# Attention and a gated convolution on one core: row sums inverted in 128 rows, last keys turned by DVE, jobs ordered by due times alone

## The chip, the cores and the metric

One core of a Trainium2 chip runs one program. The metric is the device time of one execution in microseconds; the time of a kernel is the median of its runs. The engines are TensorE (PE, with PEld for its weight loads), VectorE (DVE), ScalarE (ACT), GpSimd (POOL) and SyncE (SP), whose queue issues nearly all DMAs here.

## The reference

```python
# q, k, v: 8 batches x 8 heads x 576 x 64, float32
scores = matmul(rotate(q), rotate(k).T) / sqrt(64)
attn = exp(scores - max(scores))
attn = attn / (sum(attn) + 1e-9)
x = matmul(attn, v)                          # -> 8 x 576 x 512
gate_pre[:, s] = sum(conv_w[t] * x[:, s + t - 4] for t in range(5))
out = (1 / (1 + exp(-gate_pre)) * (x @ w_val)) @ w_out
```

## The kernel before, in words

The work is cut into 32 pairs: two heads of one batch side by side in the 128 partitions. Four pairs make a batch; then the gated block of this batch follows, in two halves of 288 positions and four chunks of 128 columns.

A pair goes through these stages. `load` brings queries and keys with their swapped halves into the single tiles `qin` and `kin`. `rope_mul` (two products with the tables), `rope_add`, `qk_hi` (a cast) and `qk_lo` (a difference) turn them into a high and a low part. `s_mm` computes the scores in five chunks c: chunks 0 to 3 have 128 queries for each of the two heads, chunk 4 is the mixed one, with the last 64 queries of both heads. For each of the nine score tiles `s_max` (DVE) takes the negative maximum into `nm`, and `s_exp` (ACT) the exponential, whose row sum goes into a column of `sums`. The exponentials have queries in partitions; the product with the values needs keys there, so they are turned.

For the first pairs (p < EARLY) and the last one PE transposes them (`t_mm`), and ACT or DVE copies the result (`t_copy`). For the others DVE transposes 32 x 32 blocks (`turn`, eight a pair, 512 keys each) into a staging tile T, and sixteen DMAs (`move`) carry the blocks to their places in the tile P. T and P come from the three buffers `big`. The last 64 of the 576 keys of both heads are transposed by PE in every pair (`th_mm`, four transposes) and copied into `pl` by `h_copy`. The mixed tile `pm` is turned by PE (`tm_mm`, `hm_mm`) and copied into `pq` by `m_copy` and `hm_copy`; `hm_mm` also transposes the row sums, to 16 rows of 128.

`r_inv` adds 1e-9 and inverts them on these 16 rows, `r_write` stores them in DRAM (`rd`), and `r_read` reads them back, spread over 64 partitions (`rb`). `pv_mm` and `pvm_mm` multiply by the values, `x_norm` and `xm_norm` multiply by the inverses. Then `x_hi`, `x_lo`, the five taps of the convolution (`tap`: the first on ACT, four on DVE), and `gate`. The gated block is `f_mm` for both matrices, with `y_mul`, `y_hi`, `y_lo` between them and `o_out`, `o_dma` at the end. The weights and taps come as 64-bit floats and are decoded at the start (`decode`).

What sets the order: every step is a job with a due time, an engine, an estimated duration, and the tokens that it reads and writes. The due time is a base, counted from the start of the pair in a period of 18.0, plus a number from the table DUE. `Plan.order` walks the jobs with estimated durations: for each engine it looks at the jobs that can start within a short time of the earliest, takes the one with the smallest due time, and of the engines' choices the earliest start. This gives one sequence of jobs, and each engine gets its part of it in this order. PICK says which engine does a job that several can do. Each engine works strictly in its row.

## Time and profile before

| what | us |
|---|---|
| median of 3 runs | 727.49 (727.17 to 730.32) |
| profiled execution, time | 730.04 |
| its span, first to last instruction | 728.2 |
| PE, DVE, ACT, POOL busy in it | 653.0, 630.7, 464.7, 423.3 |
| normalization of pair 4 starts | 153.40 |
| normalization of pair 30 starts | 677.85 |

The span is shorter than the execution's time by what lies before the first and after the last instruction. Busy time of an engine is the time in which it had at least one instruction running. In a row of the groups view, the numbers after the first bar are the busy time in us and the mean of one instruction in ns, and after the second bar the idle time of the engine just before these instructions, with what ended it. Line numbers are those of the kernel before; a name such as `ps_t` stands for all buffers of that tile.

### The profile page before, as it was taken

The numbers are of one execution on the slowest core, as the hardware profiler recorded it, in microseconds if no ns is written. First come the engines' busy times: TensorE is split into PE (matmuls) and PEld (weight loads), VectorE is DVE, ScalarE is ACT, GpSimd is POOL, SyncE is SP. The second block draws the span as 40 slices with busy tenths as digits, with TensorE's granted clock in tenths as the row PEclk, the third lists the DMA queues.
The fourth block names the chain that finished last, engine by engine and source line by source line (L and its number), as shares of the span: only waits on it lengthen the run. The fifth ranks groups of instructions, "written<-read, shape, count | busy, mean of one in ns | idle before, by whom it ended". The sixth has DMA issues, their size and how long they took to land.

```text
span 728.2 us, 14173 instructions
## 1 busy us (share of the span) xinstructions
PE 653.0 (90%) x5044; PEld 473.2 (65%) x5044; DVE 630.7 (87%) x980; ACT 464.7 (64%) x1125; POOL 423.3 (58%) x312
## 2 busy tenths in 40 slices
...
GB/s 257 66 130 186 30 101 129 114 154 220 231 226 217 206 214 195 214 213 216 225 205 186 211 203 184 213 202 214 232 222 175 221 184 222 215 187 153 49 33 66
DMA packets 52245, 129.63 MB, mean 178 GB/s; under 512 B 11184, under 2 KB 21200, under 8 KB 52176
## 3 DMA queue, kind: packets, MB, share of 16 engines
...
## 4 chain that ended last, share of the span: by engine, by line
PE 37%; DVE 31%; DMA 13%; ACT 6%; SPq 6%; issue 5%; POOL 2%; DVEq 0%; ACTq 0%; POOLq 0%
PE ps_t L472 13%; PE ps_t L377 9%; DVE nm L275 9%; PE ps_s L269 8%; DVE g L446 6%; DVE big L304 6%; SPq L309 4%; DMA kin<-in_k 4%; ACT p L288 3%; DMA v<-in_v 3%; DMA big<-big 3%; PE ps_t L380 3%; DMA rb<-rd 2%; DVE kin L233 2%; DVE rr L399 1%
## 5 line engine op out<-in xcount | busy, mean ns | idle before, releaser
L288 ACT ACTIVATE p<-ps_s,nm 128x576 f32<-128x576 f32 x256 | 188.1, 739 | 79.1 <-DVE nm L275 76.6
L275 DVE TENSOR_REDUCE nm<-ps_s 128x1 f32<-128x576 f32 x288 | 204.2, 738 | 23.4 <-PE ps_s L269 22.4
L269 PE MATMUL ps_s<-k,q 64*128 64x288 f32 x1536 | 152.0, 320 | 20.2 <-ACT k L244 8.9
L269 PEld LDWEIGHTS ps_s<-k,q 64*128 64x128 f32 x1536 | 116.6, 193 | 52.2 <-issue 21.0
L304 DVE STREAM_TRANSPOSE big<-p 128x512 f32<-128x512 f32 x216 | 142.4, 685 | 6.1 <-ACT p L288 5.9
L233 POOL TENSOR_TENSOR qin<-qin,tab 128x576 f32<-128x576 f32 x59 | 87.5, 1497 | 70.4 <-DMA qin<-in_q 64.3
L446 DVE SCALAR_TENSOR_TENSOR g<-x,cw,g 128x576 f32<-128x576 f32 (+1 forms) x132 | 125.6, 956 | 1.9 <-ACT g L443 1.7
L377 PE MATMUL ps_t<-big,v 128*64 128x512 f32 (+2 forms) x528 | 119.4, 586 | 5.5 <-DMA rd<-rr 3.2
L472 PE MATMUL ps_t<-yh,wout_hi 128*128 128x288 f32 x256 | 81.2, 317 | 4.9 <-ACT pl L213 1.8
L472 PE MATMUL ps_t<-xh,wval_hi 128*128 128x288 f32 x256 | 80.1, 313 | 3.1 <-DVE g L477 2.0
L237 POOL TENSOR_TENSOR kin<-kin 128x576 f32<-128x576 f32 (+1 forms) x32 | 51.0, 1594 | 45.9 <-DVE kin L233 38.8
L472 PE MATMUL ps_t<-yh,wout_lo 128*128 128x288 f32 x256 | 77.5, 303 | 0.0
L472 PE MATMUL ps_t<-yl,wout_hi 128*128 128x288 f32 x256 | 77.4, 302 | 0.0
L472 PE MATMUL ps_t<-xl,wval_hi 128*128 128x288 f32 x256 | 76.8, 300 | 0.0
L472 PE MATMUL ps_t<-xh,wval_lo 128*128 128x288 f32 x256 | 76.5, 299 | 0.0
L377 PEld LDWEIGHTS ps_t<-big,v 128*64 128x64 f32 x528 | 36.1, 136 | 62.1 <-issue 56.4
L433 POOL TENSOR_TENSOR xl<-x,xh 128x576 fp32r<-128x576 f32 (+1 forms) x32 | 51.5, 1608 | 41.6 <-ACT xh L429 39.9
L485 POOL TENSOR_TENSOR yl<-g,yh 128x288 fp32r<-128x288 f32 x56 | 47.2, 843 | 34.9 <-ACT yh L481 34.8
L248 POOL TENSOR_TENSOR q<-qin,q 128x576 fp32r<-128x576 f32 (+1 forms) x32 | 49.2, 1536 | 31.3 <-ACT q L244 31.3
L233 POOL TENSOR_TENSOR kin<-kin,tab 128x576 f32<-128x576 f32 x34 | 52.5, 1547 | 14.5 <-DMA kin<-in_k 14.5
L248 POOL TENSOR_TENSOR k<-kin,k 128x576 fp32r<-128x576 f32 x31 | 45.8, 1479 | 23.0 <-ACT k L244 21.9
L472 PEld LDWEIGHTS ps_t<-yh,wout_hi 128*128 128x128 f32 x256 | 49.2, 192 | 10.4 <-DVE g L477 2.6
...
## 6 DMA issues: line engine op xcount, KB each, us to landing
big<-big SPq DMA_DIRECT2D x432, 128.0 KB
...
```

The source lines that it names most:

```text
L233: eng.tensor_tensor(out=t[:, i, a:b], in0=t[:, i, a:b], in1=tabs[:, i, a:b], op=ALU.mult)
L237: eng.tensor_tensor(out=t[:, 0], in0=t[:, 0], in1=t[:, 1], op=ALU.add)
L248: eng.tensor_tensor(out=t[:, 1], in0=ins[n][:, 0, a:b], in1=t[:, 0].bitcast(F32), op=ALU.subtract)
L269: T.matmul(out=ps[:, half, 0:288], lhsT=st["q"][rows, x, c * 128:c * 128 + 128] if c < 4 else mixq[p % 2][:, x], rhs=st["k"][rows, y, k0:k ...
L275: V.tensor_reduce(out=st[f"nm{i}"], in_=st[f"s{i}"], axis=AX.XY, op=ALU.max, negate=True)
L288: A.activation(out=pd.rearrange("p (b x) -> p b x", b=2), in_=st[f"s{i}"], func=AF.Exp, bias=st[f"nm{i}"], scale=1.0, accum_out=sums[p % 2 ...
L304: V.transpose(out=t[:, :, cs.index(c), h].rearrange("p b k i -> p k b i"), in_=st[f"p{c}"][:, h, h * D:h * D + M].rearrange("p (k b i) -> ...
L377: T.matmul(out=acc[HEAD[h], 0:n], lhsT=st["v"][:, j, h, :], rhs=st["pt"][:, :, c0:c1, h, j].rearrange("p a c i -> p c a i"), start=(j == 0 ...
L433: eng.tensor_tensor(out=st["xl"][:, a:b], in0=xs[p % 2][:, 4 + a:4 + b], in1=st["xh"][:, a:b].bitcast(F32), op=ALU.subtract)
L446: V.scalar_tensor_tensor(out=g, in0=x_sb[:, a + k:b + k], scalar=w, in1=g, op0=ALU.mult, op1=ALU.add)
L472: T.matmul(out=acc[:, 0:n], lhsT=wt[w][:, kc, ds], rhs=mv, start=(kc == 0 and i == 0), stop=(kc == NCH - 1 and i == 2))
L485: eng.tensor_tensor(out=ffn[b, "l", dc, lo], in0=y, in1=ffn[b, "h", dc, lo].bitcast(F32), op=ALU.subtract)
```

## The change

1. `r_inv` works on the sums where they are, as nine columns in 128 partitions, and writes the inverses into columns 576 to 584 of `pm`, which is now a constant tile of 640 columns. `hm_mm` transposes columns 512 to 639, so the last keys of the mixed tile and the inverses are turned together; the transpose of `sums` is gone. `hm_copy` copies 96 rows to `pq`, now on DVE instead of ACT, and `r_write` reads the inverses from `pq`.
2. `turn` of the second head takes 640 columns instead of 512, so the last keys of both heads go through DVE and the moves as a ninth block of the tile P. A move carries 1152 elements a row instead of 1024. `th_mm` and `h_copy` stay only for the pairs that PE turns. `pl` and `rr` are gone.
3. `order` keeps no estimate of time: jobs whose inputs have been issued lie in a heap by their due time, and one whose buffer is not free is parked until one is. DUE has new numbers; the period is 18.5.
4. EARLY is 5 instead of 4. `yh` and `yl` have 7 buffers each instead of 8. One step of the weight decoding becomes an absolute value on ACT. PICK moves, among others, the key product with the cosine table (`kmul0`) from DVE to POOL and the output eviction `od1` from ACT to DVE.

```diff
-EARLY = 4
+EARLY = 5
-DUE = {'c0': 223.82, 'c0e': 343.31, ...
-PICK = {... 'chm': 'A', ... 'kmul0': 'V', ... 'od1': 'A', ...
+DUE = {'taps': -379.65, 'dtap': 4.77, ...
+PICK = {... 'chm': 'V', ... 'kmul0': 'G', ... 'od1': 'V', ...
-    BUFS = {"p": 3, "pm": 1, "big": 3, "pl": 2, "pq": 1, ... "yh": 8, "rb": 2, "rr": 1, "yl": 8, ...
+    BUFS = {"p": 3, "pm": 1, "big": 3, "pq": 1, ... "yh": 7, "rb": 2, "yl": 7, ...
     def order(self):
...
+        heap = [(jobs[i][0], i) for i in range(len(jobs)) if not left[i]]
+        heapify(heap)
         done = []
+        while heap:
+            i = heappop(heap)[1]
             got = []
             for inst in allocs[i]:
                 if inst not in self.slot:
                     tag = inst.split("/")[0]
+                    idle = [(freed.get(held, -1), k) for k, held in enumerate(slots[tag])
+                            if (tag, k) not in [g[1:] for g in got] and not to_come.get(held)]
+                    if not idle:
+                        parked[tag].append(i)
+                        break
+                    got.append((inst, tag, min(idle)[1]))
...
+    pm = const.tile([128, S + D], F32, name="pm")
...
-            st["pt"] = get(f"big/P{p}", [128, 4096]).rearrange("p (a c h k i) -> p a c h k i", a=4, c=4, h=2, k=4)
+            st["pt"] = get(f"big/P{p}", [128, 4608]).rearrange("p (a c k i) -> p a c k i", a=4, c=4, k=9)
...
+        k0, k1 = ((0, 4), (4, 9))[h]
+        V.transpose(out=t[:, :, cs.index(c), k0:k1].rearrange("p b k i -> p k b i"),
+                    in_=st[f"p{c}"].rearrange("p h s -> p (h s)")[:, k0 * 128:k1 * 128].rearrange("p (k b i) -> p k b i", b=4, i=32))
...
     def hm_mm(p):
-        T.transpose(out=st["bhm"][:, 0:128], in_=st["pm"][:, 448:S], identity=ident)
-        T.transpose(out=st["bhm"][0:16, 128:256], in_=sums[p % 2], identity=ident)
+        T.transpose(out=state[p]["bhm"][:, 0:128], in_=pm[:, M:S + D], identity=ident)
     def hm_copy(p, eng):
-        cast(eng, mixed(p)[D:128, M:M + 128], st["bhm"][D:128, 0:128])
+        cast(eng, mixed(p)[0:D + 32, M:M + 128], st["bhm"][0:D + 32, 0:128])
...
     def r_inv(p):
-        V.tensor_scalar(out=r, in0=st["bhm"][0:16, 128:256], scalar1=1e-9, scalar2=None, op0=ALU.add)
-        V.reciprocal(out=r, in_=r)
+        r = sums[p % 2][:, 0:9]
+        V.tensor_scalar(out=r, in0=r, scalar1=1e-9, scalar2=None, op0=ALU.add)
+        V.reciprocal(out=pm[:, S:S + 9], in_=r)
     def r_write(p, part):
-            SP.dma_start(out=st["rd"][0, 0:9 * 128]..., in_=st["rr"][0:9])
+            SP.dma_start(out=st["rd"][0, 0:9 * 128]..., in_=st["pq"][D:D + 9, M:M + 128])
...
-            lambda: V.tensor_scalar(out=hi, in0=hi, scalar1=0x7FF00000, scalar2=None, op0=ALU.bitwise_and),
+            lambda: A.activation(out=fh, in_=fh, func=AF.Abs) if eng else
+            V.tensor_scalar(out=hi, in0=hi, scalar1=0x7FF00000, scalar2=None, op0=ALU.bitwise_and),
...
-    PERIOD = 18.0
+    PERIOD = 18.5
```

Three places show how the rows of the engines change. The first is DVE's row in the middle of the run, around the inversion of one pair. `rr` are the turned sums, `big` the staging tile T, `p` the exponentials; L304 is `turn`, L275 `s_max`, L477 `y_mul`, L233 the key product `kmul0`, L446 a tap. Before:

```order
L398 TENSOR_SCALAR rr_3410<-ps_t_3411 16x128
L399 RECIPROCAL rr_3410<-rr_3410 16x128
L304 STREAM_TRANSPOSE big_3414<-p_3400 128x4x4x32
L275 TENSOR_REDUCE nm_3447<-ps_s_3416 128x1
L275 TENSOR_REDUCE nm_3459<-ps_s_3417 128x1
L477 SCALAR_TENSOR_TENSOR g_2858<-g_2858,ps_t_3441 128x288
L304 STREAM_TRANSPOSE big_3414<-p_3461 128x4x4x32 x2
L477 SCALAR_TENSOR_TENSOR g_2595<-g_2595,ps_t_3466 128x288
L233 TENSOR_TENSOR kin<-kin,tab 128x576
L446 SCALAR_TENSOR_TENSOR g_3379<-x_84,cw,g_3379 128x576
```

The same place in DVE's row after the change, where L356 and L357 are `r_inv`, L404 a tap, L376 and L380 `x_norm` and `xm_norm` of the pair before, L265 `turn`, L235 `s_max`, L435 `y_mul` and L175 the copy `hm_copy`:

```order
L356 TENSOR_SCALAR sums_87<-sums_87 128x9
L357 RECIPROCAL pm<-sums_87 128x9
L404 SCALAR_TENSOR_TENSOR g_3321<-x_85,cw,g_3321 128x576
L376 TENSOR_TENSOR x_84<-ps_t_3468,rb_3464 128x512
L265 STREAM_TRANSPOSE big_3544<-p_3532 128x4x4x32
L235 TENSOR_REDUCE nm_3560<-ps_s_3546 128x1
L380 TENSOR_TENSOR x_84<-ps_t_3564,rb_3464 128x64
L235 TENSOR_REDUCE nm_3611<-ps_s_3547 128x1
L265 STREAM_TRANSPOSE big_3544<-p_3532 128x5x4x32
L435 SCALAR_TENSOR_TENSOR g_2548<-g_2548,ps_t_3580 128x288
L175 COPY pq_3616<-ps_t_3617 96x128
```

The inversion has moved from behind PE's transpose to ahead of it, the copy follows nine rows later, every second transpose is the longer one, and the key product is no longer in the row.

The second place is PE's row around the transposes of one pair: L269 is `s_mm`, L332 `th_mm`, L361 and L362 `hm_mm`, L344 `tm_mm`. Before:

```order
L269 MATMUL ps_s_2316<-k_71,q_73 128x288
L332 MATMUL ps_t_2335<-ident,p_2207 128x128
L332 MATMUL ps_t_2335<-ident,p_2257 128x128
L361 MATMUL ps_t_2345<-ident,pm_2279 128x128
L362 MATMUL ps_t_2345<-ident,sums_85 16x128
L344 MATMUL ps_t_2356<-ident,pm_2279 128x128 x4
L269 MATMUL ps_s_2365<-k_71,q_73 128x288
```

After, with L430 `f_mm`, L321 `hm_mm` and L229 `s_mm`:

```order
L430 MATMUL ps_t_6164<-yl_5803,wout_hi 128x288
L430 MATMUL ps_t_6164<-yh_5802,wout_lo 128x288
L430 MATMUL ps_t_6164<-yh_5722,wout_hi 128x288
L430 MATMUL ps_t_6164<-yl_5723,wout_hi 128x288
L430 MATMUL ps_t_6164<-yh_5722,wout_lo 128x288
L321 MATMUL ps_t_6188<-ident,pm 128x128
L229 MATMUL ps_s_6195<-k_70,q_72 128x288
```

Of the transposes around the scores one is left here, between a block of `f_mm` and the next scores; the four of `tm_mm` follow after these scores.

The third place is POOL's row, which rotates queries and keys: L233 is `rope_mul`, L237 `rope_add`, L248 `qk_lo`, L433 `x_lo`, L485 `y_lo`. Before:

```order
L233 TENSOR_TENSOR qin<-qin,tab 128x576 x2
L237 TENSOR_TENSOR qin<-qin 128x576
L233 TENSOR_TENSOR kin<-kin,tab 128x576
L433 TENSOR_TENSOR xl_4488<-x_84,xh_4487 128x576
L248 TENSOR_TENSOR q_72<-qin,q_72 128x576
L237 TENSOR_TENSOR kin<-kin 128x576
L485 TENSOR_TENSOR yl_4544<-g_3935,yh_4543 128x288
L248 TENSOR_TENSOR k_70<-kin,k_70 128x576
```

After, where the same functions are L193, L197, L208, L391 and L443:

```order
L193 TENSOR_TENSOR qin<-qin,tab 128x576 x2
L193 TENSOR_TENSOR kin<-kin,tab 128x576 x2
L197 TENSOR_TENSOR kin<-kin 128x576
L197 TENSOR_TENSOR qin<-qin 128x576
L208 TENSOR_TENSOR k_71<-kin,k_71 128x576
L208 TENSOR_TENSOR q_73<-qin,q_73 128x576
L391 TENSOR_TENSOR xl_4180<-x_85,xh_4179 128x576
L391 TENSOR_TENSOR xl_4184<-x_84,xh_4183 128x576
L443 TENSOR_TENSOR yl_4165<-g_2845,yh_4164 128x288
```

Both key products now stand in POOL's row, and the product for xl has moved behind the rotation.

More of the change, by code (lines that the diff above doesn't have):

```diff
@@ L1 @@
 from contextlib import ExitStack
+from heapq import heapify, heappop, heappush
 import numpy as np
@@ L36 @@
 class Plan:
[L39 to L43 removed]
+    BUFS = {"p": 3, "pm": 1, "big": 3, "pq": 1, "xh": 5, "xl": 5, "g": 5, "yh": 7, "rb": 2, "yl": 7, "oo": 3, "rd": 2,
+            "ps_s": 3, "ps_t": 2, "nm": 4}
@@ L45, in __init__, with add @@
     def __init__(self):
         self.jobs = []
-    def add(self, due, engine, ns, fn, *args, r="", w="", kb=0, mode=None, port=False, hold=False):
-        self.jobs.append((due, engine, ns, fn, args, r.split(), w.split(), kb * 3.6, mode, port or engine == "G", hold))
+    def add(self, due, engine, fn, *args, r="", w=""):
+        self.jobs.append((due, engine, fn, args, r.split(), w.split()))
     def graph(self):
@@ L80, in graph, with order @@
         return [len(d) for d in deps], outs, allocs, uses
-    def order(self, due=None):
+    def order(self):
         jobs = self.jobs
-        n = len(jobs)
-        due = due or [j[0] for j in jobs]
         left, outs, allocs, uses = self.graph()
-        ready = [1000 * due[i] if jobs[i][10] else 0.0 for i in range(n)]
-        start, end = [None] * n, [0.0] * n
-        free = dict.fromkeys(self.LAG, 0.0)
-        open_jobs = {e: [] for e in free}
-        to_come, freed, self.slot = {}, {}, {}
+        to_come, freed, self.slot, self.before = {}, {}, {}, {}
         for u in uses:
@@ L95, in order @@
         slots = {tag: [None] * k for tag, k in self.BUFS.items()}
-        for i in range(n):
-            if not left[i]:
-                open_jobs[jobs[i][1]].append(i)
+        parked = {tag: [] for tag in slots}
+        heap = [(jobs[i][0], i) for i in range(len(jobs)) if not left[i]]
+        heapify(heap)
         done = []
-        moving = port = 0.0
-        mode = None
-        def earliest(i):
-            job = jobs[i]
-            t = max(ready[i], free[job[1]])
-            if job[9]:
-                t = max(t, port)
+        while heap:
+            i = heappop(heap)[1]
             got = []
@@ L161, in order @@
-        self.start, self.end = start, end
+                    idle = [(freed.get(held, -1), k) for k, held in enumerate(slots[tag])
[4 more added lines that the diff above has]
+                    got.append((inst, tag, min(idle)[1]))
+            else:
+                for inst, tag, k in got:
+                    self.slot[inst], self.before[inst] = k, slots[tag][k]
+                    slots[tag][k] = inst
+                for inst in uses[i]:
+                    to_come[inst] -= 1
+                    freed[inst] = len(done)
+                    if not to_come[inst]:
+                        tag = inst.split("/")[0]
+                        for j in parked[tag]:
+                            heappush(heap, (jobs[j][0], j))
+                        parked[tag] = []
+                done.append(i)
+                for o in outs[i]:
+                    left[o] -= 1
+                    if not left[o]:
+                        heappush(heap, (jobs[o][0], o))
@@ L162, in order @@
+        assert len(done) == len(jobs), "no job can start"
         return done
@@ L343, in tm_mm @@
         for j in range(4):
-            T.transpose(out=st["bm"][:, j * 128:(j + 1) * 128], in_=st["pm"][:, j * 128:(j + 1) * 128], identity=ident)
+            T.transpose(out=st["bm"][:, j * 128:(j + 1) * 128], in_=pm[:, j * 128:(j + 1) * 128], identity=ident)
     def mixed(p):
@@ L527, in load_taps @@
         tmp = get("oo/taps1", [128, G1])[:, 0:NCH * TAPS]
-        taps.extend(decode(st, tmp, V, whole=cw))
+        taps.extend(decode(st, tmp, whole=cw))
     wsteps, wstage = {}, {}
@@ L547, in attn_gated_ffn, with at @@
             V.memset(x_sb[:, 0:4], 0.0)
-        for s_ in sums:
-            V.memset(s_, 1.0)
+        V.memset(pm, 0.0)
         for t in mixq:
             V.memset(t.bitcast(F32), 0.0)
-    def at(key, base, e, ns, fn, *args, pick=None, **kw):
+    def at(key, base, e, ns, fn, *args, pick=None, r="", w="", kb=0, mode=None, port=False):
+        options = ns if pick else None
         if pick:
-            options = ns
             e = PICK.get(pick, e)
-            ns, kw["port"] = options[e]
+            ns, port = options[e]
             args = [ENG[e] if a == "ENGINE" else a for a in args]
-        plan.add(base + DUE.get(key, 0.0), e, ns, fn, *args, **kw)
+        plan.add(base + DUE.get(key, 0.0), e, fn, *args, r=r, w=w)
         if collect is not None:
-            collect.append((key, base, pick, options if pick else None))
+            collect.append((key, base, pick, options, ns, kb * 3.6, mode, port or e == "G"))
     def toks(f, *ranges):
@@ L578, in attn_gated_ffn @@
     for i in range(7):
-        at("dtap", 16 + 0.4 * i, "V", 150, lambda i=i: taps[i](), w="cw oo/taps0 oo/taps1", port=i in (1, 3, 5, 6), hold=True)
+        at("dtap", 16 + 0.4 * i, "V", 150, lambda i=i: taps[i](), w="cw oo/taps0 oo/taps1", port=i in (1, 3, 5, 6))
     def weights(n):
```

156 lines of the change are left out of this document (50 added, 106 removed).

## The prediction

> **What bounds the kernel now.** I read the page's engine totals first, then its chain, then the busy time in the stretch where the pairs run at an even pace.
>
> ```profile
> PE 653.0 (90%) x5044; PEld 473.2 (65%) x5044; DVE 630.7 (87%) x980; ACT 464.7 (64%) x1125; POOL 423.3 (58%) x312
> PE 37%; DVE 31%; DMA 13%; ACT 6%; SPq 6%; issue 5%; POOL 2%; DVEq 0%; ACTq 0%; POOLq 0%
> 153.40 0.69 DVE L418 TENSOR_TENSOR x<-ps_t,rb 128x512 f32<-128x512 f32 x1
> 677.85 0.69 DVE L418 TENSOR_TENSOR x<-ps_t,rb 128x512 f32<-128x512 f32 x1 [3.09 <-PE ps_t L380]
> 153.40:677.85 524.45, 497.31 (x3933) 358.17 (x3934) 472.21 (x726) 357.43 (x881) 342.46 (x253) 0.99 0.78 206
> ```
>
> The first row is the page's first part, the second its chain. The two L418 rows, from the timeline, are the normalization of pair 4 and of pair 30 (the fifth and the thirty-first to be normalized). Between them lie 26 pairs, so a pair takes 524.45 / 26 = 20.17 us. The last row is that stretch in the windows view: PE, PEld, DVE, ACT and POOL busy, the granted clock, the DMA share and GB/s. DVE is busy 472.21 of 524.45 us (90%), PE 497.31 (95%), POOL 342.46 (65%). No engine alone is the bound: the chain goes back and forth between PE and DVE, with loads between. So I cost both, and then ask whether POOL or a load is next.
>
> **DVE, part by part.** These rows, grouped by shape, carry the terms.
>
> ```profile
> L399 DVE RECIPROCAL rr<-rr 16x128 f32<-16x128 f32 x32 | 30.1, 941 | 1.1
> L398 DVE TENSOR_SCALAR rr<-ps_t 16x128 f32<-16x128 f32 x32 | 8.8, 274 | 5.0 <-PE ps_t L362 2.8 <-ACT pq L213 1.6 <-DMA v<-in_v 0.3
> L511 DVE TENSOR_SCALAR oo<-oo 128x20 int32<-128x20 int32 x1 | 0.2, 167 | 0.0
> L549 DVE MEMSET sums<- 128x16 f32 x2 | 0.1, 72 | 0.0
> L304 DVE STREAM_TRANSPOSE big<-p 128x512 f32<-128x512 f32 x216 | 142.4, 685 | 6.1 <-ACT p L288 5.9
> L233 DVE TENSOR_TENSOR kin<-kin,tab 128x576 f32<-128x576 f32 x28 | 25.9, 926 | 3.5 <-DMA kin<-in_k 3.5
> L418 DVE TENSOR_TENSOR x<-ps_t,rb 128x128 f32<-128x128 f32 x1 | 0.3, 292 | 0.4 <-PE ps_t L380 0.4
> L493 DVE TENSOR_SCALAR oo<-ps_t 128x288 f32<-128x288 f32 x4 | 1.8, 458 | 7.0 <-PE ps_t L472 7.0
> L509 DVE TENSOR_SCALAR big<-big 128x512 int32<-128x512 int32 x8 | 3.5, 437 | 0.0
> L215 DVE CAST k<-k 64x128 fp32r<-64x128 f32 x4 | 2.4, 591 | 0.1
> L215 DVE COPY pl<-ps_t 128x256 f32<-128x256 f32 x4 | 1.6, 412 | 1.4 <-PE ps_t L332 1.4
> L237 DVE TENSOR_TENSOR qin<-qin 128x576 f32<-128x576 f32 x3 | 3.4, 1147 | 0.0
> ```
>
> - Inversion: 32 x (0.941 + 0.274) = 38.9 us leave; 32 pairs of instructions on 128x9 come. No row shows that shape. The bounds are the 72 ns of a 128x16 memset and the 274 ns of L398; I take 167 ns each, from the 128x20 row, the nearest in shape with arithmetic. That is 10.7 us, net -28.2 (-34.3 to -21.4).
> - Transposes: 216 of 512 elements become 104 of 512 and 104 of 640. Eight go with pair 4, which now takes the PE route: -5.5. The longer form is between 685 ns (a fixed cost) and 856 (in proportion); I take 856, since 685 for 512 leaves little room for a fixed part: +17.8. Net +12.3 (-5.5 at the least).
> - The key product with the cosine table (`kmul0`): of 28 on DVE 8 stay: 20 x 0.926 = -18.5.
> - The copy of the turned mixed tail (`chm`) comes from ACT: 32 x 0.292 (L418's 128x128 form, also read from PSUM) = +9.3.
> - Output evictions: 4 become 16: 12 x 0.458 = +5.5.
> - Start and end: eight mask steps of the weight decoding (-3.5), four key casts (-2.4), four copies to pl (-1.6) and three adds of qin (-3.4) leave; four adds of kin (+4.6 at 1.147), a product (+1.2) and three evictions (about +1.5) come: -3.6.
>
> The sum is -28.2 + 12.3 - 18.5 + 9.3 + 5.5 - 3.6 = -23.2 us.
>
> **The port that DVE shares with POOL.** What leaves DVE lands on POOL: 20 products at 1.547 us, 30.9 us (the few adds that change places nearly cancel), so 423.3 becomes some 452 us (+6.8%). What POOL does is not free for DVE.
>
> ```profile
> L233 POOL TENSOR_TENSOR kin<-kin,tab 128x576 f32<-128x576 f32 x34 | 52.5, 1547 | 14.5 <-DMA kin<-in_k 14.5
> L446 DVE SCALAR_TENSOR_TENSOR g<-x,cw,g 128x576 f32<-128x576 f32 x124 | 121.7, 983 | 1.9 <-ACT g L443 1.7
> 494.60 0.77 DVE L446 SCALAR_TENSOR_TENSOR g<-x,cw,g 128x576 f32<-128x576 f32 x1
> 18.23 1.37 DVE L508 SCALAR_TENSOR_TENSOR oo<-oo,oo 128x20 int32<-128x20 int32 x1
> ```
>
> A tap can take 0.77 us; twenty elements, beside a POOL instruction, took 1.37. So the mean of 983 ns holds 213 ns of waiting, 26.4 us over 124 taps. With POOL work 6.8% up in a span some 3% shorter this grows by a tenth: +2.6. DVE's account becomes -20.6.
>
> The Trainium skill, page "SBUF — State Buffer", section "Who interferes with whom", says that a DVE instruction with two SBUF inputs and a GpSimd instruction shut each other out for the whole instruction. By it every two-input instruction waits on average half of a POOL instruction (0.7 us) times POOL's share, which rises by about 0.08; for 124 taps and as many other two-input instructions at most that is an estimated +14 us, and the forecast would be some 11 us later. The 20 elements that took 1.37 us agree with the rule; the mean tap, which waits 0.21 us and not 0.7 x 0.65 = 0.46, says that it is met half as often.
>
> **PE.** 104 of the 128 transposes of the last keys (L332) and all 32 of the row sums (L362) leave; 32 for pair 4 (L318) come. The matmuls that use the last keys stay, now out of the big tile.
>
> ```profile
> L332 PE MATMUL ps_t<-ident,p 128*128 128x128 f32 x128 | 28.8, 304 | 18.0 <-ACT p L288 11.3 <-DVE x L422 4.7 <-DVE rr L398 0.7
> L318 PE MATMUL ps_t<-ident,p 128*128 128x128 f32 x160 | 28.4, 322 | 10.5 <-DVE x L418 4.5 <-ACT big L213 2.4 <-DVE big L215 1.7
> L362 PE MATMUL ps_t<-ident,sums 128*16 128x128 f32 x32 | 9.0, 281 | 0.0
> L332 PEld LDWEIGHTS ps_t<-ident,p 128*128 128x128 f32 x128 | 14.1, 144 | 30.1 <-ACT p L288 12.4 <-issue 5.8 <-DVE x L422 4.5
> L318 PEld LDWEIGHTS ps_t<-ident,p 128*128 128x128 f32 x160 | 21.0, 163 | 17.2 <-ACT big L213 4.9 <-DVE x L418 4.6 <-DVE big L215 2.4
> L362 PEld LDWEIGHTS ps_t<-ident,sums 128*16 128x16 f32 x32 | 3.0, 93 | 0.0
> ```
>
> By PE's busy time this is -104 x 0.225 + 32 x 0.178 - 9.0 = -26.7 us; by the weight loads beneath it -104 x 0.110 (14.1 us for 128) + 32 x 0.131 - 3.0 = -10.3. I take the larger end, since the first row also has 18.0 us in which PE stood idle ahead of these transposes, and that wait goes with them; it is not in the sum.
>
> The Trainium skill, page "Perfetto Trace Analysis", section "Identifying the Most-Contended Engine", holds matmul busy time for a bad measure of how full TensorE is, and LDWEIGHTS busy time for a good one. By it PE is 65% full, its term is -10.3, and the weighted sum below would be -16 instead of -23. The chain, which puts 37% on PE, speaks against taking it for slack.
>
> **ACT, the row-sum path, buffers and DMA.**
>
> ```profile
> L213 ACT COPY pl<-ps_t 128x256 f32<-128x256 f32 x60 | 22.1, 368 | 13.8 <-PE ps_t L332 13.4
> L213 ACT COPY pq<-ps_t 64x128 f32<-64x128 f32 x32 | 8.4, 262 | 6.8 <-PE ps_t L362 4.3 <-DVE rr L398 1.9
> 304.40 1.96 DMA rd<-rr
> 450.29 4.54 DMA rb<-rd
> big<-big SPq DMA_DIRECT2D x432, 128.0 KB
> ```
>
> ACT loses these two groups (30.5 us) and 12 output evictions, and gains the evictions of pair 4 and the decoding steps; it carries 6% of the chain, so I count nothing for it. The inverse now goes DVE, PE, DVE, SP instead of PE, DVE, SP: a copy more. On DVE the copy stands nine rows behind the inverse, and behind it wait taps and maxima if PE is late; on SP the write of the inverses waits for it, and behind that stand the next key load, the value load and the reads of the inverses. What hides it: the normalization that needs the inverses stands 24 DVE rows, at 472.21 / 726 = 0.65 us each some 16 us, behind the copy, against 1.96 + 4.54 us for write and read in the longer cases on the chain. If that cover is gone, DVE waits in every pair for what exceeds it. Nothing is counted. One buffer fewer for yh and yl binds only the eighth group of a batch, after the output matmuls that free the first have been issued; nothing again. The 416 moves carry 144 KB instead of 432 with 128 KB: 4.6 MB more of 129.63. With a shorter span the DMA share goes from 0.78 to some 0.83, which is room left, but loads may land later (a rival).
>
> **The sum.** DVE -20.6, PE -26.7. They take turns on the chain, 31 to 37, so I weight them: (31 x 20.6 + 37 x 26.7) / 68 = 23.9, rounded down to 23, since some of the gain will meet the next wait. Against the profiled execution: span 728.2 - 23 = 705.2, and with the 1.84 us that lie outside the span (730.04 - 728.2) 707.0. The median of the runs is 727.49, 2.55 below that execution, so the forecast is 727.5 - 23 = 704.5.
>
> **Rivals.**
>
> *The rotation of queries and keys becomes the bound (slower).* `kin` and `qin` are single tiles: the next load waits for the last instruction that reads the tile.
>
> ```profile
> POOL kin L237 <- DVE kin L233: 38.8, 18, 11.5
> POOL qin L233 <- DMA qin<-in_q: 64.3, 18, 8.9
> 452.55 0.54 SPq L219 DMA_DIRECT2D qin<-in_q  x1
> 457.00 1.41 POOL L233 TENSOR_TENSOR qin<-qin,tab 128x576 f32<-128x576 f32 x1 [8.95 <-DMA qin<-in_q]
> 471.02 1.43 POOL L248 TENSOR_TENSOR q<-qin,q 128x576 fp32r<-128x576 f32 x1
> 472.47 0.35 SPq L219 DMA_DIRECT2D qin<-in_q  x1
> 210.62 6.58 DMA kin<-in_k
> 571.43 7.70 DMA kin<-in_k
> ```
>
> In this round the load was issued at 452.55, POOL began at 457.00 (4.45 us), the last reader ended at 472.45, and the next load went out at 472.47: 19.92 us, nearly the pace of 20.17. From POOL's first instruction to the last that is 15.45 us. After the change the second key product joins (+1.43), the product for xl, which stood among these, is issued behind them (-1.43), and the wait for DVE's key product goes (38.8 / 18 = 2.2 us a time): 13.3 plus the load. For this rival speaks that POOL already waits 64.3 us for query loads; against it, that with 4.45 us for the load the loop is 17.7 and binds nothing (the forecast's pace is 20.17 - 23 / 32 = 19.45). At 6.9 us it equals today's pace. At 7.70, which the chain has once, it is 21.0, and 26 pairs cost 26 x 0.83 = 22 us more than now: 749.
>
> *The same loop eats part of the gain (faster).* At 6.58 us the loop is 19.88 and 26 pairs save 7.5 us: 720.
>
> *PE's waits go too (faster).* If the 18.0 us of idle time before L332 leave with the transposes, it is 704.5 - 18 = 686.5. Against it: what PE waited for (ACT's exponentials, DVE) is still needed by the next instruction in its row.
>
> *The order does not deliver it (no change).* Jobs come out by due times alone, without estimated durations at that point. DVE was idle 52.2 us of the stretch; if the new order leaves some 23 more, the work saved becomes idle time: 727. Against it: the new DVE row repeats almost unchanged from pair to pair.
>
> **How the numbers follow.** Forecast 0.52 (694 to 713); PE's waits gone as well 0.12; part of it eaten 0.15; no change 0.07; slower by the rotation loop 0.14. The range of 8 in 10 leaves out the slower case and half of the 686.5 case: 688 to 728. Half a per cent (3.6 us) is about what a measurement can tell from no change; faster by more: 0.52 + 0.12 + 0.15 = 0.79, within 0.07, slower 0.14.
>
> **What the new profile should show.** RECIPROCAL on 128x9 at 0.1 to 0.3 us in place of 941 ns; transposes of 640 elements near 856 ns; DVE busy about 610 us and PE about 626; POOL about 452 us, with no wait for a DVE key product; taps with a mean near 1.0 us; a pace of 19.4 to 19.5 us between normalizations. I am wrong if the chain is led by loads of `qin` or `kin`, if DVE waits for `rb` in most pairs, or if DVE's idle time has grown by what its work shrank.

## The result, and the profile after

| | before | after |
|---|---|---|
| median of the runs, us | 727.58 (727.17 to 730.32) | 701.3 (698.02 to 702.38) |
| ratio, 95% interval | | 0.9623 [0.9582, 0.9665] |
| profiled execution and its span, us | 730.04, 728.2 | 702.26, 700.5 |
| pair 10 to pair 30, us a pair | 20.25 | 19.22 |

The kernel became faster by 26 us; forecast were 704.5, range 688 to 728. Medians, here and in the table of experiments, are of all runs, while the ratios leave out five runs in a slower state (one each of e4, f3 and g4, two of g1). First the page's first part and its chain after the change:

```profile
PE 633.7 (90%) x4940; PEld 463.5 (66%) x4940; DVE 621.2 (89%) x985; ACT 446.8 (64%) x1050; POOL 451.4 (64%) x329
PE 41%; DVE 28%; SPq 10%; ACT 8%; DMA 7%; issue 5%; POOL 2%; DVEq 0%; ACTq 0%; POOLq 0%
```

PE's busy time fell by 19.3 us, DVE's by 9.5, ACT's by 17.9; POOL's rose by 28.1. The chain still goes between PE and DVE; DMA transfers have 7% of it instead of 13%, and SP's queue, which issues the moves, has 10% instead of 6%.

The next two rows are the windows view from the normalization of pair 10 to that of pair 30, before and after (PE, PEld, DVE, ACT, POOL, clock, DMA share, GB/s):

```profile
272.85:677.85 405.00, 383.14 (x3019) 276.17 (x3020) 360.84 (x553) 274.43 (x677) 256.20 (x192) 0.99 0.77 203
```

```profile
265.70:650.15 384.45, 368.11 (x2925) 267.61 (x2924) 359.21 (x563) 255.16 (x606) 283.17 (x206) 0.99 0.86 226
```

Twenty pairs take 20.55 us less; the other 7 us come before pair 10. In these pairs DVE is busy as long as before (359.21 against 360.84 us), but its idle time fell from 44.2 to 25.2 us. In PE's row it is the other way round: PE is busy 15.0 us less and idle 5.5 us less. So in these pairs the gain is idle time in DVE's row and mostly busy time in PE's.

Over the whole run DVE is busy 9.5 us less and idle 18.2 us less (97.5 before, 79.3 after). Here are its groups by shape to which the prediction gave a price (the first number behind the bar is busy us, the second the mean in ns):

```profile
L404 DVE SCALAR_TENSOR_TENSOR g<-x,cw,g 128x576 f32<-128x576 f32 x124 | 139.5, 1125 | 0.8 <-ACT g L401 0.4 <-issue 0.3
L265 DVE STREAM_TRANSPOSE big<-p 128x640 f32<-128x640 f32 x104 | 83.0, 812 | 0.0
L265 DVE STREAM_TRANSPOSE big<-p 128x512 f32<-128x512 f32 x104 | 71.8, 691 | 0.0
L356 DVE TENSOR_SCALAR sums<-sums 128x9 f32<-128x9 f32 x32 | 21.7, 677 | 3.6 <-ACT pm L248 3.6
L175 DVE COPY pq<-ps_t 96x128 f32<-96x128 f32 x32 | 8.4, 262 | 6.3 <-PE ps_t L321 6.3
L451 DVE TENSOR_SCALAR oo<-ps_t 128x288 f32<-128x288 f32 x16 | 7.0, 435 | 6.5 <-PE ps_t L430 6.4
L357 DVE RECIPROCAL pm<-sums 128x9 f32<-128x9 f32 x32 | 6.9, 216 | 1.1
L193 DVE TENSOR_TENSOR kin<-kin,tab 128x576 f32<-128x576 f32 x8 | 6.0, 750 | 0.0
```

The busy times of all DVE groups add up to 674.4 us before and 675.2 after. That sum is above DVE's busy time, because the record of an instruction begins some 0.07 us before that of its forerunner ends, where the two stand back to back. Between groups such moments count twice, and after the change there are more of them. So the sum hides the 9.5 us, and the span less the sum is not idle time. Both readings agree that the smaller part of the 27.7 us is time that DVE's instructions take.

Some of the longest waits after the change, and then ACT's waits for the maxima before it:

```profile
POOL qin L193 <- DMA qin<-in_q: 71.0, 22, 7.8
ACT p L248 <- DVE nm L235: 68.9, 88, 5.0
ACT pm L248 <- DVE nm L235: 40.0, 23, 2.9
POOL xl L391 <- ACT xh L387: 56.6, 22, 29.0
PEld ps_s L229 <- ACT p L248: 51.2, 54, 5.8
```

```profile
ACT p L288 <- DVE nm L275: 76.6, 85, 8.7
ACT pm L288 <- DVE nm L275: 27.0, 14, 3.9
```

POOL's wait for DVE's key product is gone, and its wait for query loads is a little longer (64.3 before). ACT waits less for the maxima of the eight tiles `p`, but more for those of the mixed tile `pm`: 108.9 us together, against 103.6 before.

Why the addition of 1e-9 on nine columns takes 677 ns on average can be read in the timeline. Both pieces are from one pair, the first of DVE, the second of POOL (start, duration):

```profile
398.56 1.00 DVE L356 TENSOR_SCALAR sums<-sums 128x9 f32<-128x9 f32 x1
399.60 0.22 DVE L357 RECIPROCAL pm<-sums 128x9 f32<-128x9 f32 x1
399.73 1.91 DVE L404 SCALAR_TENSOR_TENSOR g<-x,cw,g 128x576 f32<-128x576 f32 x1
```

```profile
398.13 1.40 POOL L193 TENSOR_TENSOR kin<-kin,tab 128x576 f32<-128x576 f32 x1
399.61 1.41 POOL L197 TENSOR_TENSOR kin<-kin 128x576 f32<-128x576 f32 x1
```

The addition ends at 399.56, when POOL's product has ended (399.53). The tap behind it ends at 401.64, 0.62 us after POOL's next instruction (401.02), as if it had begun only then; a tap that begins while POOL is idle takes 0.81 us on average (56 of the 124). The tile view gives the spread of the two small instructions (min/median/max in ns):

```profile
L356 DVE TENSOR_SCALAR sums<-sums x32: 148/738/1392, 34.1 to 647.7; 128x9 f32<-128x9 f32 x32
L357 DVE RECIPROCAL pm<-sums x32: 215/216/217, 34.4 to 647.9; 128x9 f32<-128x9 f32 x32
```

Of the 32 additions, 25 end 0.03 us after a POOL instruction that was running when they began, and take 278 ns or more; the other seven take 148 to 176 ns. So the addition waits for POOL; the inversion beside it, with one input as well, never does.

### The profile page after: what moved, and what is told of

Same layout as the page of the kernel before. It is cut to its first block, busy times and chain, and to the rows that moved or that the text cites. A ratio compares the mean times of both kernels' runs of the same rounds, so it can differ in the third digit from the quotient of the medians.

```text
span 700.5 us, 13923 instructions
## 1 busy us (share of the span) xinstructions
PE 633.7 (90%) x4940; PEld 463.5 (66%) x4940; DVE 621.2 (89%) x985; ACT 446.8 (64%) x1050; POOL 451.4 (64%) x329
## 3 DMA queue, kind: packets, MB, share of 16 engines
q1 hardware_dynamic: 50864, 132.86, 69.9%
## 4 chain that ended last, share of the span: by engine, by line
PE 41%; DVE 28%; SPq 10%; ACT 8%; DMA 7%; issue 5%; POOL 2%; DVEq 0%; ACTq 0%; POOLq 0%
PE ps_t L430 18%; PE ps_s L229 10%; SPq L270 10%; DVE nm L235 8%; DVE big L265 7%; PE ps_t L336 6%; DMA big<-big 5%; DVE g L404 5%; ACT p L248 4%; PE ps_t L339 2%; DVE g L435 1%; PE ps_t L306 1%; DMA qin<-in_q 1%; PE ps_t L279 1%; DVE x L376 1%
## 5 line engine op out<-in xcount | busy, mean ns | idle before, releaser
L248 ACT ACTIVATE p<-ps_s,nm 128x576 f32<-128x576 f32 x256 | 189.2, 742 | 69.8 <-DVE nm L235 68.9
L235 DVE TENSOR_REDUCE nm<-ps_s 128x1 f32<-128x576 f32 x288 | 205.8, 739 | 24.2 <-PE ps_s L229 22.8
L229 PE MATMUL ps_s<-k,q 64*128 64x288 f32 x1536 | 154.4, 322 | 31.0 <-ACT p L248 18.0
L229 PEld LDWEIGHTS ps_s<-k,q 64*128 64x128 f32 x1536 | 118.4, 194 | 85.0 <-ACT p L248 46.0
L265 DVE STREAM_TRANSPOSE big<-p 128x512 f32<-128x512 f32 x208 | 150.6, 751 | 0.0
L404 DVE SCALAR_TENSOR_TENSOR g<-x,cw,g 128x576 f32<-128x576 f32 (+1 forms) x132 | 143.6, 1088 | 1.0 <-ACT g L401 0.4
L193 POOL TENSOR_TENSOR qin<-qin,tab 128x576 f32<-128x576 f32 x58 | 87.1, 1518 | 75.3 <-DMA qin<-in_q 71.0
L336 PE MATMUL ps_t<-big,v 128*64 128x512 f32 (+2 forms) x528 | 122.2, 590 | 2.1 <-PE ps_s L229 1.3
L430 PE MATMUL ps_t<-yh,wout_hi 128*128 128x288 f32 x256 | 80.4, 314 | 4.6 <-DVE x L376 2.9
L193 POOL TENSOR_TENSOR kin<-kin,tab 128x576 f32<-128x576 f32 (+1 forms) x55 | 79.1, 1451 | 7.0 <-DMA kin<-in_k 7.0
L391 POOL TENSOR_TENSOR xl<-x,xh 128x576 fp32r<-128x576 f32 (+1 forms) x33 | 46.2, 1408 | 56.6 <-ACT xh L387 56.6
L430 PE MATMUL ps_t<-xh,wval_hi 128*128 128x288 f32 x256 | 79.3, 310 | 1.9 <-DVE x L376 1.0
L430 PE MATMUL ps_t<-yl,wout_hi 128*128 128x288 f32 x256 | 77.0, 301 | 2.6 <-POOL yl L443 2.5
L430 PE MATMUL ps_t<-xl,wval_hi 128*128 128x288 f32 x256 | 76.8, 300 | 0.0
L430 PE MATMUL ps_t<-xh,wval_lo 128*128 128x288 f32 x256 | 76.8, 300 | 0.0
L430 PE MATMUL ps_t<-yh,wout_lo 128*128 128x288 f32 x256 | 76.4, 298 | 0.0
L208 POOL TENSOR_TENSOR q<-qin,q 128x576 fp32r<-128x576 f32 (+1 forms) x32 | 51.5, 1611 | 37.6 <-ACT q L204 29.5
L336 PEld LDWEIGHTS ps_t<-big,v 128*64 128x64 f32 x528 | 33.1, 136 | 52.7 <-issue 48.7
L197 POOL TENSOR_TENSOR qin<-qin 128x576 f32<-128x576 f32 x31 | 54.6, 1762 | 7.4 <-DVE qin L193 7.4
L208 POOL TENSOR_TENSOR k<-kin,k 128x576 fp32r<-128x576 f32 x31 | 45.8, 1478 | 20.2 <-ACT k L204 19.6
L430 PEld LDWEIGHTS ps_t<-yh,wout_hi 128*128 128x128 f32 x256 | 49.8, 195 | 10.6 <-DVE x L376 3.7
L443 POOL TENSOR_TENSOR yl<-g,yh 128x288 fp32r<-128x288 f32 x56 | 51.2, 918 | 6.8 <-ACT yh L439 6.8
```

Source lines behind the costliest of these rows:

```text
L193: eng.tensor_tensor(out=t[:, i, a:b], in0=t[:, i, a:b], in1=tabs[:, i, a:b], op=ALU.mult)
L197: eng.tensor_tensor(out=t[:, 0], in0=t[:, 0], in1=t[:, 1], op=ALU.add)
L208: eng.tensor_tensor(out=t[:, 1], in0=ins[n][:, 0, a:b], in1=t[:, 0].bitcast(F32), op=ALU.subtract)
L229: T.matmul(out=ps[:, half, 0:288], lhsT=st["q"][rows, x, c * 128:c * 128 + 128] if c < 4 else mixq[p % 2][:, x], rhs=st["k"][rows, y, k0:k ...
L235: V.tensor_reduce(out=st[f"nm{i}"], in_=st[f"s{i}"], axis=AX.XY, op=ALU.max, negate=True)
L248: A.activation(out=pd.rearrange("p (b x) -> p b x", b=2), in_=st[f"s{i}"], func=AF.Exp, bias=st[f"nm{i}"], scale=1.0, accum_out=sums[p % 2 ...
```

## The experiments

Two theories stood against each other. W: the gain comes from less work on DVE and PE, as the prediction summed it. O: it comes from the order, which leaves less idle time. Ratios are to the kernel before, with 95% intervals; the change itself has 0.9623 [0.9582, 0.9665].

| run | base and edit | median us | ratio |
|---|---|---|---|
| e1_old_work | after, the old inversion, last keys and engines | 788.0 | 1.0799 [1.0724, 1.0874] |
| e2_old_keys | after, last keys by PE again | 760.77 | 1.0408 [1.0352, 1.0464] |
| e3_old_inverse | after, sums turned and inverted in 16 rows again | 709.95 | 0.9708 [0.965, 0.9766] |
| e4_kmul_dve | after, first key product on DVE again | 744.43 | 1.017 [1.0103, 1.0236] |
| f1_no_add | after, without the addition | 693.3 | 0.952 [0.9456, 0.9584] |
| f2_new_work_old_plan | before's planner and table, all new work | 813.03 | 1.1173 [1.1102, 1.1244] |
| f3_inverse_old_plan | before, new inversion alone | 754.22 | 1.0343 [1.0264, 1.0422] |
| f4_keys_old_plan | before, last keys by DVE alone | 785.87 | 1.079 [1.0718, 1.0862] |
| g1_short_inverse | before, inversion of 9 elements, not 128 | 721.83 | 0.9843 [0.9792, 0.9894] |
| g2_less_work | before, three works shortened | 719.73 | 0.9852 [0.9798, 0.9905] |
| g3_more_dve | after, one more inversion a pair on DVE | 706.28 | 0.9669 [0.9625, 0.9714] |
| g4_more_pe | after, two more transposes a pair on PE | 700.77 | 0.9567 [0.9514, 0.9619] |

**Undoing parts under the new order.** The due times stay as the change has them; the work goes back.

*e1_old_work*: the old bodies of `turn`, `th_mm`, `h_copy`, `hm_mm`, `r_inv`, `r_write`, and

```diff
-PICK = {... 'chm': 'V', ... 'kmul0': 'G', ... 'od1': 'V', ...
+PICK = {... 'chm': 'A', ... 'kmul0': 'V', ... 'od1': 'A', ...
```

> The order of the change (heap by due times, its table of due times, five early pairs, the absolute value in the decoding) with the work of before: row sums turned and inverted on 16 rows, last keys turned by PE, kmul0 on DVE, hm_copy and od1 on ACT. Theory W (the 26 us come from less work on DVE and PE): DVE busy back at about 630 us, PE at about 650, time 722 to 730. Theory O (they come from the order, which leaves less idle time): DVE busy about 630 as well, but its idle time in the even stretch stays near 6 to 7% instead of 11%, time 704 to 712.

Measured: 788.0, far above both. The waits and a group of DVE:

```profile
DVE rr L357 <- ACT pq L173: 76.3, 27, 5.9
POOL xl L392 <- ACT xh L388: 121.1, 25, 31.4
L357 DVE TENSOR_SCALAR rr<-ps_t 16x128 f32<-16x128 f32 x32 | 8.9, 279 | 80.0 <-ACT pq L173 76.3 <-PE ps_t L322 3.6
```

DVE stands idle for 80.0 us ahead of the old inversion. It comes in DVE's row where the new one stands, and the new one needs nothing from PE and waits 3.6 us for ACT. The order knows no durations, and so it cannot move the inversion to where its input is ready. This run doesn't measure the work; it measures a misfit.

*e2_old_keys*:

```diff
-        for cl in ((0, 1), (2, 3)):
-            cl = tuple(c for c in cl if c not in cs)
+        for g in R2:
...
+                at(f"th{c}" + ph, t + 3.6 * c + 7.5, "PE", 218, th_mm, p, g, ...
```

> The changed kernel with the last keys turned by PE again (four transposes and two copies of 256 columns on ACT a pair, 512-element transposes on DVE, moves of 1024 elements). Theory W: DVE loses 104 x 0.121 = 12.6 us of work, PE gets back about 23 us by its busy time and ACT 22 us; PE was 96% busy in the even stretch, so 10 to 20 us slower, 711 to 721. Theory O with DVE as the bound: DVE has 0.5 us a pair less to do, 690 to 698.

Measured: 760.77; both wrong again. Of its waits:

```profile
DVE nm L235 <- PE ps_s L229: 47.1, 47, 2.6
DVE pq L175 <- PE ps_t L319: 39.3, 21, 3.6
```

In the changed kernel these are 22.8 and 6.3 us. DVE waits for PE, which has the old transposes of the last keys in its row again.

*e3_old_inverse*:

```diff
+        T.transpose(out=st["bhm"][0:16, 128:256], in_=sums[p % 2], identity=ident)
...
-        V.reciprocal(out=pm[:, S:S + 9], in_=r)
+        V.tensor_scalar(out=r, in0=state[p]["bhm"][0:16, 128:256], scalar1=1e-9, scalar2=None, op0=ALU.add)
+        V.reciprocal(out=r, in_=r)
```

> The changed kernel with the row sums turned and inverted on 16 rows again (one more transpose on PE, 0.27 + 0.94 us on DVE in place of 0.68 + 0.22). Theory W and DVE as the bound: 32 x 0.31 = 10 us more on DVE and 9 us on PE, 708 to 714. Rival, the inversion is off the path: 699 to 704.

Measured: 709.95, in the range of W. But DVE does not have more to do:

```profile
L407 DVE SCALAR_TENSOR_TENSOR g<-x,cw,g 128x576 f32<-128x576 f32 x124 | 122.1, 985 | 0.0
L360 DVE RECIPROCAL rr<-rr 16x128 f32<-16x128 f32 x32 | 30.1, 941 | 1.1
L359 DVE TENSOR_SCALAR rr<-ps_t 16x128 f32<-16x128 f32 x32 | 8.5, 267 | 4.0 <-PE ps_t L324 4.0
```

The old inversion takes 38.6 us against 28.6, and the taps 122.1 against 139.5: with the long inversion DVE is busy 615.9 us, 5.3 less than with the short one, and the kernel is 6 us slower by the ratios (0.0085 x 727.58; their intervals overlap a little), 9 by the medians. What the short one saves in its own row it more than pays at the port. PE is busy 7.0 us more here (640.7), which would fit the 6 us, but was not tried apart.

*e4_kmul_dve*:

```diff
-PICK = {... 'kmul0': 'G', ...
+PICK = {... 'kmul0': 'V', ...
```

> The changed kernel with the product kmul0 on DVE again for the 27 later pairs. Theory DVE is the bound: 27 x 0.75 to 0.93 us = 20 to 25 us more on DVE, less what DVE no longer waits at the shared port because POOL has 39 us less to do (taps from 1.125 back to about 1.0 us, 12 us): 8 to 15 us slower, 709 to 716. Rival, the port gives back all of it: 699 to 704.

Measured: 744.43, above both. The product's own row says a part of why:

```profile
L193 DVE TENSOR_TENSOR kin<-kin,tab 128x576 f32<-128x576 f32 x35 | 40.8, 1166 | 20.8 <-DMA kin<-in_k 20.4 <-POOL qin L193 0.3
ACT pm L248 <- DVE nm L235: 89.2, 26, 6.3
```

At the place that the due time gives it, the product stalls DVE for 20.4 us until key loads land, and the maxima queued behind it keep ACT waiting (40.0 us in the changed kernel).

**The new work under the old planner.** The planner of before estimates durations and fits its order to them, so it should adapt.

*f2_new_work_old_plan*: all of the new work, with the old `Plan`, DUE, PERIOD and EARLY.

> All of the new work (inversion on 128 rows, last keys by DVE, first key product on POOL, mixed copy and one output copy on DVE) with the planner of before, which estimates durations and fits an order to them, and with its table. If the gain needs both (less work and an order that is fitted to it), the planner refits and most of the gain comes: 700 to 712 us. Rival (the due-time order alone carries it, the work counts little): 720 to 735 us.

*f3_inverse_old_plan*: the kernel before with

```diff
-        at("thm" + ph, t + 17.3, "PE", 217, hm_mm, ...
-        at("rinv" + ph, t + 17.8, "V", 400, r_inv, p, r=f"ps_t/{p}n", w=f"rr/{p}")
+        at("rinv" + ph, t + 17, "V", 350, r_inv, p, r=toks(f"sums{par}#@", range(9)), ...
+        at("thm" + ph, t + 17.8, "PE", 150, hm_mm, p, r=f"pm/{p} pm/{p}#r", ...
```

and the new bodies of `hm_mm`, `hm_copy`, `r_inv` and `r_write`.

> The kernel before with the inversion on 128 rows alone, its planner refitting. DVE loses 30.1 us of 941 ns inversions and their additions and gains 28.6 us at the most if the addition waits at the port as in the changed kernel (677 and 216 ns): 722 to 728 us by the durations measured there. If the addition waits less than in the changed kernel (POOL has 423 us of work instead of 451): 712 to 720. Rival (the longer path through the mixed copy holds the normalization up): 730 to 742.

*f4_keys_old_plan*: the kernel before with the new `turn`, `move` and `h_copy`, and no `th_mm` where DVE turns.

> The kernel before with the last keys turned by DVE alone, its planner refitting. DVE +12.3 us, PE -10 to -27 us, ACT loses its copies of the last keys (18 us). If DVE is the bound of the even pairs: 733 to 742 us, slower. If PE's waits for its copies were: 714 to 724 us. Between: nothing, 725 to 730.

Measured: 813.03, 754.22 and 785.87. Each is slower than every theory had it. The waits for the maxima in f2 and f4, 76.6 us in the kernel before:

```profile
ACT p L290 <- DVE nm L277: 118.8, 101, 10.5
```

```profile
ACT p L288 <- DVE nm L275: 105.8, 107, 5.0
```

In f3 this wait is 69.9 us, no longer than before; there PE stands idle for 95.5 us (75.2 before). So the old planner, with its own table of due times, does not fit itself to the new work. Nothing from e1 to e4 or f2 to f4 can be read as the price of a part; each shows what it costs when order and work don't fit.

**Changing work without moving anything.** That leaves one way to weigh work: keep an order that fits, and make single instructions shorter, or add some for which nobody waits.

*g1_short_inverse*, in the kernel before:

```diff
-        V.reciprocal(out=r, in_=r)
+        V.reciprocal(out=r[:, 0:9], in_=r[:, 0:9])
```

> The kernel before, in exactly its order, with the inversion shortened to 9 of its 128 elements (the rest of the sums stays uninverted). DVE has 32 x 0.73 = 23 us less to do, nothing else is moved. If DVE's work were the bound of the kernel before: 704 to 710 us. If DVE and PE share it, as the chain of waits had it: 713 to 720. If the kernel is held by the fit of its order (waits that do not move with an engine's work): 723 to 729.

*g2_less_work* adds to it

```diff
+        if n == "k" and i == 0 and p >= EARLY and eng is V:
+            b = a + 64
...
-        for c in range(2):
+        for c in range(1):
             T.transpose(out=st[f"bh{g}"][:, c * 128:(c + 1) * 128], ...
```

> The kernel before, in exactly its order, with three works shortened: the inversion as in the run beside it, the first key product on DVE to 64 of 576 columns in the pairs from the fifth on, and the last keys turned by one transpose of two on PE (the copies and everything behind them stay; keys and last keys are partly wrong data). DVE -40 us, PE -18.6 us, about the work that the change takes from these engines, with nothing added and nothing moved. If less work makes the gain: 697 to 706 us. If the new order makes it: 716 to 726.

Measured: 721.83 and 719.73, by the ratios 11 us below the kernel before in both (727.58 x 0.0157 and x 0.0148); the intervals allow 7 to 15. Engine totals of g1, then of g2:

```profile
PE 650.9 (90%) x5044; PEld 472.0 (66%) x5044; DVE 616.9 (86%) x980; ACT 463.5 (64%) x1125; POOL 419.4 (58%) x312
```

```profile
PE 646.3 (90%) x4980; PEld 469.6 (66%) x4980; DVE 602.2 (84%) x980; ACT 462.9 (65%) x1125; POOL 416.1 (58%) x312
```

DVE is busy 13.8 us less in g1 and 28.5 us less in g2, where PE has 6.7 us less too; the time is the same. (In g2 the product on 64 of 576 columns still takes 554 ns, presumably since it waits for POOL.) The first 14 us of DVE's work are worth some 11; of the next 15 nothing can be seen. A part of it may be hidden by the granted clock, which was 0.962 to 0.971 in g2's runs and 0.974 to 0.979 in the four of g1 that its ratio uses. The kernel before, run beside them, took 727.21 us at 0.981 and 736.42 at 0.961, so 0.01 of clock may go with some 5 us (an estimate from these two runs). So this much less work, in the old order, gives some 11 of the 26 us. It is not all the work that the change takes away: PE is busy 6.7 us less in g2 and 19.3 in the change, ACT 1.8 and 17.9.

*g3_more_dve*, in the changed kernel:

```diff
         V.reciprocal(out=pm[:, S:S + 9], in_=r)
+        V.reciprocal(out=spare, in_=spare)
```

> The changed kernel, in exactly its order, with one more inversion of 16x96 elements per pair on DVE behind the inversion, about 0.74 us, 24 us in all, for which nobody waits. DVE's share of the bound after the change: 722 to 727 us if DVE alone bounds; 710 to 717 if it shares the bound with PE; 702 to 705 if DVE's idle time (79 us) takes it.

*g4_more_pe*, in the changed kernel:

```diff
+        for j in range(1, 3):
+            T.transpose(out=state[p]["bhm"][:, j * 128:(j + 1) * 128], in_=pm[:, j * 128:(j + 1) * 128], identity=ident)
```

> The changed kernel, in exactly its order, with two more transposes of 128x128 per pair on PE behind the mixed tile's last turn, 64 x 0.29 = 18.6 us in all, for which nobody waits. 718 to 722 us if PE alone bounds; 707 to 714 if PE shares the bound with DVE; 701 to 704 if PE's idle time (67 us) takes it.

Measured: 706.28 and 700.77. The engine totals, the taps and the added group of g3, then the totals and the added group of g4:

```profile
PE 632.6 (90%) x4940; PEld 462.3 (66%) x4940; DVE 629.6 (90%) x1018; ACT 447.2 (64%) x1050; POOL 450.6 (64%) x329
L406 DVE SCALAR_TENSOR_TENSOR g<-x,cw,g 128x576 f32<-128x576 f32 x124 | 128.0, 1032 | 0.0
L359 DVE RECIPROCAL spare<-spare 16x96 f32<-16x96 f32 x32 | 21.8, 682 | 0.0
```

```profile
PE 629.9 (91%) x5004; PEld 459.8 (66%) x5004; DVE 622.7 (90%) x985; ACT 447.1 (64%) x1050; POOL 450.6 (65%) x329
L323 PE MATMUL ps_t<-ident,pm 128*128 128x128 f32 x64 | 12.2, 272 | 0.0
```

Twenty-two us more on DVE cost 3 us by the ratios and 5 by the medians, and the ratios' intervals overlap. Half of it came back from the taps, which fell from 1125 to 1032 ns (139.5 to 128.0 us), presumably since POOL got done while the spare inversion ran. So after the change, too, the time does not follow DVE's work. Twelve us more on PE cost nothing measurable, but this is a weak test: PE's busy time in all is 3.8 us below that of the change although 12.2 were added, and the granted clock of this profiled execution was 0.990 against 0.976. Two runs of g4, at 0.977 and 0.980, took 704.2 and 703.0 us; the change's four, at 0.976 to 0.980, took 698.0 to 702.4. Whether PE's work sets the time, g4 does not decide.

**A better version.** *f1_no_add*:

```diff
-        r = sums[p % 2][:, 0:9]
-        V.tensor_scalar(out=r, in0=r, scalar1=1e-9, scalar2=None, op0=ALU.add)
-        V.reciprocal(out=pm[:, S:S + 9], in_=r)
+        V.reciprocal(out=pm[:, S:S + 9], in_=sums[p % 2][:, 0:9])
```

> The changed kernel without the addition of 1e-9 ahead of the inversion (each sum is at least 1, so the addition does nothing to it). It takes away the 32 instructions of 677 ns mean, 21.7 us of DVE time, most of which were spent waiting for POOL at the shared port. Theory W (DVE's work bounds the even pairs, 93.4% busy): 687 to 695 us, since some 15 of the 20 even pairs' waits are saved and a part of the wait moves on to the next tap. Rival (the wait only stands in for a later one: the tap behind it meets the same POOL instruction): 698 to 703, the taps' mean up from 1125 to 1200 ns or more.

Measured: 693.3, the fastest of all, 1.0% below the change by the ratios (their intervals just touch). Its totals, chain and taps:

```profile
PE 630.7 (91%) x4940; PEld 459.2 (66%) x4940; DVE 593.1 (85%) x953; ACT 446.7 (64%) x1050; POOL 452.0 (65%) x329
PE 51%; DVE 16%; DMA 12%; ACT 6%; POOL 5%; SPq 5%; issue 3%; DVEq 0%; ACTq 0%; POOLq 0%
L402 DVE SCALAR_TENSOR_TENSOR g<-x,cw,g 128x576 f32<-128x576 f32 x124 | 132.5, 1069 | 3.8 <-ACT g L399 3.8
```

DVE is busy 28.1 us less, and the time falls by 8, in W's range. The taps got shorter, not longer, so the wait did not move on to them; but DVE is now idle for 101 us instead of 79, and its share of the chain fell from 28% to 16%. So the number fits W, but its reason, that DVE's work is the bound, is not borne out. A part of the 8 us may be the granted clock, 0.978 to 0.994 in these runs and 0.976 to 0.980 in those of the change.

**PE's row, a rival that is left.** This table sets the span of the profiled executions against the idle time in PE's and DVE's rows (span less busy time), for the kernels whose order fits:

| kernel | span, us | PE idle | DVE idle |
|---|---|---|---|
| before | 728.2 | 75.2 | 97.5 |
| g1 | 719.9 | 69.0 | 103.0 |
| g2 | 716.6 | 70.3 | 114.4 |
| e3 | 707.4 | 66.7 | 91.5 |
| g3 | 701.5 | 68.9 | 71.9 |
| after | 700.5 | 66.8 | 79.3 |
| g4 | 695.2 | 65.3 | 72.5 |
| f1 | 694.3 | 63.6 | 101.2 |

PE's idle time stays within 12 us while DVE's moves by 42: the span goes with PE's busy time much more closely than with DVE's. In the runs whose order does not fit, PE is idle for 88.8 to 132.8 us. PE's busy time is not its work alone (f1 runs the same 4940 instructions on PE as the change, in 3.0 us less), so the table does not show that PE sets the time. But no run excludes that PE's 19.3 us make most of the gain.

## Why the prediction was right, and where it was wrong

The time was right (701.3 for 704.5), and the sum of 23 us near the 26 measured. That is in good part luck: with the busy times that came (DVE 9.5 us less, PE 19.3), the prediction's own weights give (31 x 9.5 + 37 x 19.3) / 68 = 14.8 us.

- *Inversion, -28.2 forecast.* 38.9 us became 21.7 + 6.9 = 28.6: -10.3, outside the bounds. The step that failed is the price of 167 ns for an addition on 128x9, from one 128x20 row. The kernel before had another such row, on the same shape, which the prediction passed over:

```profile
L506 DVE TENSOR_SCALAR oo<-oo 128x20 int32<-128x20 int32 x1 | 1.4, 1372 | 0.0
```

  The inversions alone came within the bounds (216 ns); the additions took 677 ns on average, and 25 of the 32 ended with a POOL instruction.
- *Port, +2.6 forecast.* The taps went from 121.7 to 139.5 us, +17.8, so the step that scaled their wait with POOL's busy time fell short by a factor of seven: taps that begin while POOL is idle take 0.80 us before and 0.81 after, but those that begin beside a POOL instruction went from 49 to 68 of 124. Thirteen of them begin beside the key addition (L197) and take 1.82 us each; before, 3 did. So it matters where POOL's work lies, not only how much there is. The Trainium skill, page "SBUF — State Buffer", section "Who interferes with whom", from which the prediction estimated +14, was nearer; but those 14 us are for the taps and as many other instructions, 7 for the taps alone, and by the weights they would have moved the forecast by 5 us, not 11. The Trainium skill counts `tensor_scalar`, in the same section, among the operations that can take the shared ports, and says that a DVE instruction with at most one SBUF input, outside the modes that use two ports, does not contend; the additions at 148 to 1392 ns and the inversions at 215 to 217 agree with both. The prediction left that out.
- *Transposes, +12.3:* 83.0 + 71.8 - 142.4 = +12.4. The long form took 812 ns, not 856; by counts and means the term is +8.3, and the rest is overlap of records that the busy time of the 216 leaves out. *Key product, -18.5:* 25.9 to 6.0, -19.9. *Copy, +9.3:* +8.4. *Evictions, +5.5:* +5.2. These came about as priced. *Start and end, -3.6:* the other groups lost 12.8 us, some 11 of them in the decoding, which the prediction had at -3.5.
- *DVE, -20.6 in all.* Busy time fell by 9.5. The added waits for POOL, 17.8 us at the taps and some 17 at the additions (an estimate, if one alone takes 0.15 us), took back most of what the work lost. The larger part of the gain in DVE's row is idle time, 18.2 us, which the prediction let stay as it was.
- *PE, -26.7 by busy time.* It fell by 19.3, PEld by 9.7 (-10.3 forecast). The groups of the transposes lost 32.5 us of busy time, more than forecast, but PE's other groups gained 8.0. With PE's term by weight loads the weights give 15 us, not the 16 of the prediction; the time fell by 26, but since it isn't shown whether PE's work sets it, this bears out neither measure.
- *Weights 31 to 37 on the two terms.* g1 to g3 show that DVE's work is not turned into time at a fixed rate here: 14 us less on DVE gave some 11, twice as much gave no more that could be seen, 22 us more cost 3 to 5.
- *The row-sum path, nothing.* Right: DVE's wait for `rb`, 8.2 + 3.9 us before, is 0.4 after.
- *DMA and the rotation loop (a rival, 749).* The share rose to 0.86 (0.83 forecast) and POOL's wait for queries from 64.3 to 71.0 us; the chain has only 1% on query loads, so the loop did not lead, at a pace of 19.22. It has little room: in 8 of the 18 rounds from 265 to 650 us the load went out as soon as POOL's last reader had ended, before in 9 of 19.
- *"The order does not deliver it" (727).* The opposite came: DVE's idle time shrank, by 18 us.

What is shown: a shorter inversion alone gives some 11 us in the old order (g1; 7 to 15 by its interval), and in DVE's row the change saves mostly idle time. The other 15 us are what is left over, not a measurement. They may come from the new order, or from the work on PE and ACT that g2 did not take away. The new order with the old work is slower than both kernels (e1), so it could not be weighed by itself. Which of the two it is, and which of the moved jobs closes the gaps, stays open.
